# A reordered first phase in a retention, ELU and maxout chain on one core

## The chip, the core and the metric

The kernel runs on one core of a Trainium2 chip. TensorE (PE) multiplies matrices into PSUM, VectorE (DVE), ScalarE (ACT) and GpSimd (POOL) work element by element, SyncE (SP) issues most transfers from memory. Each engine takes its own instructions strictly in order; semaphores hold an instruction back until what it needs is there. The metric is the device time of the kernel in microseconds, as a median of runs. One more execution was profiled, and all rows come from that one.

## The reference, cut to what matters

```python
# 4 batches, 8 heads, 768 tokens, 64 wide; gamma and scale are constants
for t in range(S):                                   # retention
    state = gamma * state + outer(k[:, :, t], v[:, :, t])
    y[:, :, t] = scale * (q[:, :, t] @ state)
x = y as (3072 tokens, 512)
h = x @ w_in                                         # 512 -> 2048
g = where(h > 0, h, exp(min(h, 0)) - 1)              # ELU
x = g @ w_out                                        # 2048 -> 512
h = max(x @ w1, x @ w2, x @ w3)                      # 512 -> 768, maxout
out = h @ w_out2                                     # 768 -> 512
```

The weights are float64 in memory.

## The kernel before

**Retention by chunks.** A chunk is 128 tokens of one batch, all heads; there are 24. For a chunk TensorE makes scores (keys by queries), VectorE multiplies them with a decay mask (`a`), TensorE multiplies the masked scores with the values and adds what the state of earlier chunks gives (`past`). The outer products of decayed keys (`kd`) and values go into the next state (`update` on TensorE, `carry` on VectorE and GpSimd). GpSimd also scales queries (`queries_of`, `qd`) and keys (`keys_of`, `kd`). The result of four chunks is one block `x` of 512 tokens, held as a high part `xh` (rounded by ScalarE) and a low part `xl` (the rest, by VectorE). Chunks 0 to 3 go through the `wide_` functions (heads in one piece of 128), later ones through `open_chunk` (scores, update, mask), `values`, `finish` and `ready` (carry, `qd`, the next `kd`), in pieces of 64. In `values`, ScalarE writes a `guard` column that the second part of `past`, in `finish`, waits for.

**Weights.** A weight of the first layer, number f of 16, is 128 columns of `w_in` and 128 rows of `w_out`, and comes in two halves of 512 KB: half 2f for `w_in`, half 2f + 1 for `w_out`. Float64 is taken apart by hand: `cv_bits(n)` (ScalarE, L337), `cv_rest(n)` (VectorE, three operations, L344, L347 and L350), `cv_high(n)` (ScalarE, L361), `cv_low(n)` (VectorE, L366). A raw half lies in one of two buffers (`stage`), and `cv_rest(n)` issues the load of half n + 2.

**Steps.** `h1(b, f)` multiplies weight f with block b (12 matmuls of 512 columns into `hp`, L396); ScalarE and VectorE make ELU of it, `Exp`, `Relu`, `e` (L403, L404, L407), and split it into `gh` (ScalarE, L408) and `gl` (VectorE, L411). `o1(b, f)` multiplies these with the other half of the weight into four accumulators `acc` (12 matmuls, L430). A step is one `h1` and one `o1`; in the loop `h1` of the next step stands ahead of `o1`. Steps run in groups (b, from f, to f): a group accumulates, and at its end `x2_out` takes the accumulators away. Blocks 0 and 1 share the first 32 steps, so that a weight is used twice while the next ones are converted: before, in seven groups, with partial sums kept in a tile (`part`) and added to at the end of later groups. `third` puts chunks 8 to 11 between steps 14 and 31.

**What sets the order.** On TensorE, VectorE, ScalarE, GpSimd and SP the order of this phase is the order of the code, until the last block of the first layer; from there a scheduler decides. Loads go through one queue of SP, in order.

Of the kernel before, what the change touches and what calls it, by code (L numbers as in the profile page):

```python
# [34 lines left out]
def kernel(ctx: ExitStack, tc: tile.TileContext, qkv0, qkv, wa, wb, dmask, qdec, cols, out):  # L35
# [221 lines left out]
    def wide_scores(c):  # L257
        x = raw_t[c]
        sc = sc_t[c] = [ps_acc.tile([P, NPAIR, P], F32, tag="acc", name="sc") for _ in range(2)]
        for p in range(NPAIR):  # L260
            for r in range(2):
                nc.tensor.matmul(
                    sc[r][:, p, :], x[rows(r), p, 1, :], x[rows(r), p, 0, :], start=p == 0, stop=p == NPAIR - 1
                )

    def wide_mask(c):
# [3 lines left out]
        for r in range(2):  # L270
            nc.vector.tensor_tensor(
                out=a[:, r], in0=sc[r], in1=dmask_sb.rearrange("j (p r) i -> j r p i", r=2)[:, r], op=ALU.mult
            )
# [163 lines left out]
    def x2_out(b, f0, f1, keep):  # L437


        if b < 2:  # L440
            if b not in part_t:
                part_t[b] = ld.tile([P, KDM, BLK], F32, tag="r", name="part")
            o = part_t[b]
            o = o if isinstance(o, list) else [o[:, m] for m in range(KDM)]
            for m in range(KDM):
                if f0:
                    nc.vector.tensor_tensor(out=o[m], in0=acc_t[b][m], in1=o[m], op=ALU.add)
                elif m % 2 == 0:
                    nc.scalar.copy(o[m], acc_t[b][m])
                else:  # L450
                    nc.vector.tensor_copy(o[m], acc_t[b][m])
                if not keep:
                    nc.sync.dma_start(out=x2d[m, :, b * BLK:(b + 1) * BLK], in_=o[m])
            if not keep:
                del part_t[b]
# [289 lines left out]
    for c in range(CB):  # L745
        wide_scores(c)
        wide_mask(c)
        if c == 0:
            junk(8)
        if c == 2:  # L750
            cv_bits(0)
            cv_rest(0)
            load(5)
        if c == 3:
            cv_high(0)
            wide_rest(2)
            cv_low(0)
        if c:
            queries_of(c)
# [233 lines left out]
```

## Time and profile before

| | us |
|---|---|
| median of 3 runs | 1018.33 (1015.37 to 1021.66) |
| the profiled execution | 1016.3 |
| its span | 1014.5 |
| TensorE busy | 985.0 (97%) |
| VectorE busy | 606.2 (60%) |
| ScalarE busy | 348.9 (34%) |
| GpSimd busy | 67.1 (7%) |

The span is the time from the first to the last instruction that the profile shows. Matmuls are pipelined and overlap, so a busy TensorE is not yet one at its peak; idle time of an engine is what no instruction covers, and the profile says what ended it. The granted clock is the share of its full 2.4 GHz that TensorE had.

### The profile page before, as it was taken

The numbers are of one execution on the slowest core, as the hardware profiler recorded it, in microseconds if no ns is written. First come the engines' busy times: TensorE is split into PE (matmuls) and PEld (weight loads), VectorE is DVE, ScalarE is ACT, GpSimd is POOL, SyncE is SP. The second block draws the span as 40 slices with busy tenths as digits, with TensorE's granted clock in tenths as the row PEclk, the third lists the DMA queues.
The fourth block names the chain that finished last, engine by engine and source line by source line (L and its number), as shares of the span: only waits on it lengthen the run. The fifth ranks groups of instructions, "written<-read, shape, count | busy, mean of one in ns | idle before, by whom it ended". The sixth has DMA issues, their size and how long they took to land.

```text
span 1014.5 us, 18210 instructions
## 1 busy us (share of the span) xinstructions
PE 985.0 (97%) x7616; PEld 841.5 (83%) x7616; DVE 606.2 (60%) x1187; ACT 348.9 (34%) x669; POOL 67.1 (7%) x68
## 2 busy tenths in 40 slices
PE   7889999999999999999999999999999999999997
PEld 4667887777888888888888887888999999899996
DVE  2867888744333323333335887997875676757764
ACT  1445555533333333333334665432221121211211
POOL 2410001021111110111100000000000000000000
PEclk9999999999999999999999999999999999999999
DMA  9913364454211211121102444302001020110101
GB/s 236 237 59 103 104 188 161 136 182 127 88 43 43 84 43 42 43 84 43 43 1 87 143 145 146 105 1 83 2 26 58 2 78 6 42 43 1 43 1 42
DMA packets 59010, 79.70 MB, mean 79 GB/s; under 512 B 5168, under 2 KB 40240, under 8 KB 58928
## 3 DMA queue, kind: packets, MB, share of 16 engines
q1 hardware_dynamic: 53168, 68.05, 22.7%
q10 hardware_dynamic: 5760, 10.49, 2.8%
q8 instruction: 60, 0.98, 0.4%
q14 instruction: 22, 0.18, 0.1%
HBM read 63.84 MB, written 14.68 MB: 77 GB/s over the span
## 4 chain that ended last, share of the span: by engine, by line
PE 74%; DVE 13%; DMA 5%; ACT 4%; issue 2%; SPq 1%; POOL 1%; ACTq 0%; DVEq 0%; POOLq 0%
PE hp L612 19%; PE hp L396 19%; PE acc L430 19%; PE acc L661 8%; PE hp L501 5%; DMA raw<-in_wb 3%; DVE t L347 2%; DVE xl L586 1%; ACT gh L408 1%; DVE t L350 1%; DVE e L407 1%; DVE t L619 1%; PE xs L217 1%; PE xs L160 1%; DVE gl L411 1%
## 5 line engine op out<-in xcount | busy, mean ns | idle before, releaser
L396 PE MATMUL hp<-xh,w 128*128 128x512 f32 x768 | 243.7, 390 | 3.8 <-ACT w L361 2.9
L612 PE MATMUL hp<-xh,w 128*128 128x256 f32 x1260 | 232.5, 283 | 2.0 <-DVE e L619 1.6
L430 PE MATMUL acc<-gh,w 128*128 128x512 f32 x768 | 206.4, 397 | 5.6 <-ACT gh L408 3.1
L612 PEld LDWEIGHTS hp<-xh,w 128*128 128x128 f32 x1260 | 198.1, 191 | 4.0 <-issue 1.4
L612 PE MATMUL hp<-xl,w 128*128 128x256 f32 x630 | 178.9, 284 | 1.4 <-DVE xl L586 1.4
L430 PEld LDWEIGHTS acc<-gh,w 128*128 128x128 f32 x768 | 142.7, 189 | 39.8 <-ACT gh L408 4.6
L396 PEld LDWEIGHTS hp<-xh,w 128*128 128x128 f32 x768 | 143.7, 188 | 35.3 <-ACT w L361 4.3
L407 DVE SCALAR_TENSOR_TENSOR e<-e,hp 128x512 f32<-128x512 f32 x96 | 65.8, 685 | 175.9 <-ACT e L404 175.2
L396 PE MATMUL hp<-xl,w 128*128 128x512 f32 x384 | 141.9, 390 | 0.7 <-DVE xl L252 0.7
L612 PEld LDWEIGHTS hp<-xl,w 128*128 128x128 f32 x630 | 120.0, 191 | 4.2 <-DVE xl L586 2.9
L403 ACT ACTIVATE e<-hp 128x512 f32<-128x512 f32 x96 | 57.2, 596 | 171.7 <-PE hp L396 169.2
L430 PE MATMUL acc<-gl,w 128*128 128x512 f32 x384 | 110.9, 390 | 0.3 <-DVE gl L411 0.3
L411 DVE TENSOR_TENSOR gl<-e,gh 128x512 fp32r<-128x512 f32 x96 | 67.3, 701 | 55.9 <-ACT gh L408 54.9
L661 PE MATMUL acc<-w,gh 128*128 128x512 f32 x288 | 90.6, 391 | 0.0
L408 ACT CAST gh<-e 128x512 fp32r<-128x512 f32 x96 | 59.5, 619 | 81.0 <-DVE e L407 79.3
L619 DVE TENSOR_TENSOR t<-hp,m 128x256 f32<-128x256 f32 (+1 forms) x90 | 45.9, 510 | 68.7 <-PE hp L612 68.1
L396 PEld LDWEIGHTS hp<-xl,w 128*128 128x128 f32 x384 | 72.0, 188 | 16.3 <-DVE xl L252 1.0
L430 PEld LDWEIGHTS acc<-gl,w 128*128 128x128 f32 x384 | 72.2, 188 | 16.0 <-DVE gl L411 0.8
L631 ACT COPY m<-hp 128x256 f32<-128x256 f32 x45 | 16.8, 373 | 189.0 <-PE hp L612 115.0
L661 PEld LDWEIGHTS acc<-w,gh 128*128 128x128 f32 x288 | 53.9, 188 | 10.0
L404 ACT ACTIVATE e<-e 128x512 f32<-128x512 f32 x96 | 60.7, 632 | 2.8
L661 PE MATMUL acc<-w,gl 128*128 128x512 f32 x144 | 56.5, 392 | 1.0 <-DVE gl L651 1.0
(100 smaller groups left out, 1048.3 us busy)
## 6 DMA issues: line engine op xcount, KB each, us to landing
...
```

The costliest lines, as they stand in the source:

```text
L347: nc.vector.scalar_tensor_tensor(out=t, in0=hi, scalar=-0x80000000, in1=t, op0=ALU.bitwise_and, op1=ALU.bitwise_or)
L396: nc.tensor.matmul(hp, w[:, pw, kk * P:(kk + 1) * P], x[px][:, kk, :], start=k == 0, stop=k == len(order) - 1,)
L403: nc.scalar.activation(e, hp, ACTF.Exp)
L404: nc.scalar.activation(e, e, ACTF.Relu, scale=-1.0, bias=1.0)
L407: nc.vector.scalar_tensor_tensor(out=e, in0=e, scalar=-1.0, in1=hp, op0=ALU.mult, op1=ALU.max)
L408: nc.scalar.copy(gh, e)
L411: nc.vector.tensor_tensor(out=gl, in0=e, in1=f32(gh), op=ALU.subtract)
L430: nc.tensor.matmul(acc_t[b][m], w[:, p[0], 512 + m * P:512 + (m + 1) * P], g[p[1]], start=f == f0 and p == first, stop=f == f1 - 1 and p = ...
L501: nc.tensor.matmul(hp, w[:, pw, c0:c0 + P], x[px][:, kk, :], start=k == 0, stop=k == 3 * KDM - 1)
L612: nc.tensor.matmul(o, ws[i][:, pw, kk * P:(kk + 1) * P], xs[i][px][:, kk, :], start=first and k == 0, stop=last and k == 5,)
L619: nc.vector.tensor_tensor(out=out, in0=a, in1=c, op=ALU.add)
L661: nc.tensor.matmul(acc_t[NB + b][m], g[px][:, m * P:(m + 1) * P], w[:, pw, 512:1024], start=f == 0 and i == 0, stop=f == KF2 - 1 and i == 2,)
```

## The change

It rewrites the first phase, up to step 31.

- The wide chunks: scores go into four accumulators and are masked in four pieces; `update` stands ahead of the mask, and the state is made apart (`wide_state`).
- Chunks 4 to 7 go one at a time between `h1(0, k)` and `o1(0, k)`, for k of 2 to 5 (a "cycle" below); before, several of them stood between the first two steps.
- Two halves are converted in each of these cycles, so that a new weight is ready for each step of block 0.
- Blocks 0 and 1 take turns in four groups: 7, 9, 9 and 7 steps. The sums of the first two groups go to memory and come back by `renew`.
- Halves of weights whose f is no multiple of 3 (below 12) are loaded into the pool `ld` in pairs; so up to six halves are on their way. `dmask` is loaded ahead of the second part of chunk 0, the halves 0, 2, 1, 3 behind chunk 3.

```diff
     def wide_scores(c):
-        sc = sc_t[c] = [ps_acc.tile([P, NPAIR, P], F32, tag="acc", name="sc") for _ in range(2)]
+        sc = sc_t[c] = [[ps_acc.tile([P, 2, P], F32, tag="acc", name="sc") for _ in range(2)] for _ in range(2)]
...
     def load_half(n):
+        f, cc = n // 2, slice(n % 2 * 512, (n % 2 + 1) * 512)
+        if f % 3 and f < 12:
+            if f not in pairs_of:
+                pairs_of[f] = ld.tile([P, 2, 512, 2], I32, tag="r", name="raw")
+            r = pairs_of[f][:, n % 2]
+        else:
             r = stage.tile([P, 512, 2], I32, tag="raw", name="raw")
...
+    def load_next(n):
+        f = n // 2
+        if f % 3 and f < 12:
+            if n % 2 and f + 3 < 12:
+                load_half(n + 5)
+                load_half(n + 6)
+        elif f < 12:
+            load_half(n + 6)
+        else:
+            load_half(n + 2)
...
-    groups = [(0, 0, 2), (1, 0, 4), (0, 2, 6), (1, 4, 8), (0, 6, 11), (1, 8, KFF), (0, 11, KFF)]
+    groups = [(0, 0, 7), (1, 0, 9), (0, 7, KFF), (1, 9, KFF)]
...
+    nc.sync.dma_start(out=dmask_sb, in_=dmask)
     load(0, 1)
-    nc.sync.dma_start(out=dmask_sb, in_=dmask)
     load(1)
     nc.sync.dma_start(out=qdec_sb, in_=qdec)
     load(2)
-    load_half(0)
     load(3)
-    load_half(1)
+    for h in (0, 2, 1, 3):
+        load_half(h)
     load(4)
+    load_half(4)
+    load_half(5)
+    load(5)
...
     for c in range(CB):
         wide_scores(c)
+        wide_update(c)
+        if c == 0:
+            junk(7)
         wide_mask(c)
-        if c == 0:
-            junk(8)
...
-    h1(0, 0, [(ready, 4), (cv_bits, 2)], [(cv_low, 1)], [(open_chunk, 4), (cv_high, 1)])
-    values(4)
-    cv_rest(2)
-    o1(0, 0, 0, 2)
-    open_chunk(5)
-    finish(4)
-    ready(5)
...
+    h1(0, 0, [(cv_low, 1)], [], [(cv_high, 1)])
+    cv_bits(3)
+    later(False)
+    nc.scalar.copy(dmask_sb[rows(1), :, 0:HC], dmask_sb[rows(1), :, HC:P])
+    cv_rest(3)
+    load(7)
+    h1(0, 1, [(cv_low, 3)], [], [(cv_high, 3)])
+    o1(0, 0, 0, 7)
+    open_chunk(4)
+    o1(0, 1, 0, 7)
+    cv_bits(4)
+    cv_rest(4)
+    cv_high(4)
+    ready(4)
+    cv_bits(5)
+    cv_low(4)
+    cv_rest(5)
+    for k in range(2, 6):
+        h1(0, k, [(cv_low, 2 * k + 1)], [], [(cv_high, 2 * k + 1)])
+        c = k + 2
+        values(c)
+        if c + 1 < EARLY:
+            open_chunk(c + 1)
+        finish(c)
+        if c + 1 < EARLY:
+            ready(c + 1)
+        o1(0, k, 0, 7)
+        cv_bits(2 * k + 2)
+        cv_rest(2 * k + 2)
+        cv_high(2 * k + 2)
+        cv_bits(2 * k + 3)
+        cv_low(2 * k + 2)
+        cv_rest(2 * k + 3)
+    h1(0, 6, [(cv_low, 13)], [], [(cv_high, 13)])
...
+        if i == split - 11:
+            renew(0)
```

VectorE before, around chunks 5 and 6 and the step (0, 1): `e` and `gl` are ELU of that step, `w<-t,w` is `cv_low`, `a` the mask of a chunk, `xl` its low part, `dmask_sb` and `state` its carry, `t` the pieces of `cv_rest`.

```order
L407 SCALAR_TENSOR_TENSOR e<-e,hp 128x512 [waits Activation_49]
L411 TENSOR_TENSOR gl<-e,gh 128x512 [waits Activation_49]
L366 TENSOR_TENSOR w<-t,w 128x512
L172 TENSOR_TENSOR a<-xs,dmask_sb 128x256 [waits PE_49] x2
L252 TENSOR_TENSOR xl<-xs,xh 128x4x64 [waits Activation_49] x2
L200 COPY dmask_sb<-xs 128x4x64
L207 TENSOR_TENSOR state_90<-xs,dmask_sb 128x256 [waits DVE_49]
L172 TENSOR_TENSOR a<-xs,dmask_sb 128x256 [waits PE_49] x2
L252 TENSOR_TENSOR xl<-xs,xh 128x4x64 [waits Activation_49] x2
L205 TENSOR_TENSOR dmask_sb<-xs,dmask_sb 128x4x64 [waits Pool_49]
L207 TENSOR_TENSOR state_91<-xs,dmask_sb 128x256 [waits DVE_49]
```

VectorE now, from `e` of the step (0, 3), in the cycle k = 3; the names are the same.

```order
L427 SCALAR_TENSOR_TENSOR e<-e,hp 128x512 [waits Activation_49]
L386 TENSOR_TENSOR w<-t,w 128x512 [waits Activation_49]
L431 TENSOR_TENSOR gl<-e,gh 128x512 [waits Activation_49]
L172 TENSOR_TENSOR a<-xs,dmask_sb 128x256 [waits PE_49] x2
L252 TENSOR_TENSOR xl<-xs,xh 128x4x64 [waits Activation_49] x2
L200 COPY dmask_sb<-xs 128x4x64
L207 TENSOR_TENSOR state_90<-xs,dmask_sb 128x256 [waits DVE_49]
L364 TENSOR_SCALAR t<-t 128x512 [waits Activation_49]
L367 SCALAR_TENSOR_TENSOR t<-raw,t 128x512 [waits DMAHW7_49,DVE_49]
L370 SCALAR_TENSOR_TENSOR t<-raw,t 128x512 [waits DVE_49]
L386 TENSOR_TENSOR w<-t,w 128x512 [waits Activation_49]
```

One chunk stands behind a step, where two stood, and the conversion of the next weight stands behind that chunk, in the same cycle.

TensorE now, from the end of `o1(0, 1)` into the cycle k = 2: `acc` is `o1`, `hp` is `h1`, `xs<-a,x` the values of chunk 4.

```order
L450 MATMUL acc<-gh,w 128x512 x4
L416 MATMUL hp<-xh,w 128x512 [waits Activation_49]
L416 MATMUL hp<-xh,w 128x512 x3
L416 MATMUL hp<-xl,w 128x512 x4
L416 MATMUL hp<-xh,w 128x512 [waits DVE_49]
L416 MATMUL hp<-xh,w 128x512 x3
L230 MATMUL xs<-a,x 64x64
```

TensorE before, from the end of `finish(4)` into `h1(0, 1)` and the values of chunk 5:

```order
L396 MATMUL hp<-xh,w 128x512 [waits DVE_49,Activation_49]
L396 MATMUL hp<-xh,w 128x512 x3
L396 MATMUL hp<-xl,w 128x512 x4
L396 MATMUL hp<-xh,w 128x512 [waits DVE_49]
L396 MATMUL hp<-xh,w 128x512 x3
L230 MATMUL xs<-a,x 64x64 [waits PE_49]
```

In both, `h1` begins behind a wait for ScalarE (`cv_high`). Now this comes once in each cycle, directly behind `o1` of the cycle before.

SP before, from the last part of chunk 2 on (`x` is a chunk, `raw` a half of a weight):

```order
L102 DMA x<-in_qkv 128x4x256
L324 DMA raw<-in_wa 128x1024
L86 DMA x<-in_qkv 64x4x128 x2
L86 DMA x<-in_qkv 64x4x256
L102 DMA x<-in_qkv 128x4x256
L324 DMA raw<-in_wa 128x1024
```

SP now, from the same place:

```order
L102 DMA x<-in_qkv 128x4x256
L86 DMA x<-in_qkv 64x4x128 x2
L86 DMA x<-in_qkv 64x4x256
L102 DMA x<-in_qkv 128x4x256
L335 DMA raw<-in_wa 128x1024 x4
```

Half 0 moved from ahead of chunk 3 to behind it, and three more halves follow it.

## Rows read from the trace of the kernel before

**Rows 1.** Three stretches: length, busy time of each engine, granted clock, DMA.

```profile
0.00:86.30 86.30, 71.83 (x902) 53.89 (x903) 52.18 (x94) 29.07 (x58) 20.63 (x22) 0.98 0.66 169
86.30:218.50 132.20, 129.03 (x733) 103.77 (x732) 101.27 (x167) 69.57 (x122) 7.84 (x7) 1.00 0.47 150
218.50:1014.50 796.00, 784.12 (x5983) 683.86 (x5982) 452.79 (x927) 250.21 (x490) 38.66 (x39) 1.00 0.18 57
```

**Rows 2.** Waits of TensorE up to 230 us: total, times, longest.

```profile
PE xo L282 <- DVE a L271: 5.7, 8, 2.7
PE hp L396 <- ACT w L361: 2.9, 4, 1.3
```

**Rows 3.** Timeline of TensorE: start, duration, operation, [idle before, releaser].

```profile
32.35 1.19 PE L396 MATMUL hp<-xh,w 128*128 128x512 f32 x4
...
45.08 1.21 PE L396 MATMUL hp<-xh,w 128*128 128x512 f32 x4 [1.28 <-ACT w L361]
...
48.07 0.69 PE L230 MATMUL xs<-a,x 64*64 64x64 f32 x32
...
50.21 0.63 PE L160 MATMUL xs<-x 64*64 64x64 f32 x27 [0.88 <-DVE e L407]
...
51.76 0.74 PE L430 MATMUL acc<-gh,w 128*128 128x512 f32 x2
...
83.62 0.39 PE L396 MATMUL hp<-xh,w 128*128 128x512 f32 x1
...
86.34 1.07 PE L430 MATMUL acc<-gh,w 128*128 128x512 f32 x4
```

**Rows 4.** Timelines of ScalarE (half 0) and GpSimd (keys of chunk 3).

```profile
23.80 0.69 ACT L337 ACTIVATE t<-raw 128x512 f32<-128x512 f32 x1 [2.53 <-DMA raw<-in_wa]
...
28.25 1.04 POOL L138 TENSOR_TENSOR kd<-x,cols_sb 128x512 f32<-128x512 f32 x1 [4.24 <-DMA x<-in_qkv]
```

**Rows 5.** Timeline of VectorE: first and last piece of one `cv_rest`.

```profile
59.44 0.43 DVE L344 TENSOR_SCALAR t<-t 128x512 int32<-128x512 int32 x1 [1.65 <-ACT t L337]
...
60.62 0.69 DVE L350 SCALAR_TENSOR_TENSOR t<-raw,t 128x512 uint32<-128x512 uint32 x1
```

**Rows 6.** Timeline of ScalarE behind `h1` at 45.08: `Exp` and a `cv_high`.

```profile
48.17 0.60 ACT L403 ACTIVATE e<-hp 128x512 f32<-128x512 f32 x1 [2.57 <-PE hp L396]
...
49.43 0.63 ACT L361 CAST w<-t 128x512 fp32r<-128x512 f32 x1
```

**Rows 7.** Timeline of VectorE behind the same `h1`.

```profile
49.47 0.69 DVE L407 SCALAR_TENSOR_TENSOR e<-e,hp 128x512 f32<-128x512 f32 x1 [0.56 <-ACT dmask_sb L240]
50.84 0.69 DVE L411 TENSOR_TENSOR gl<-e,gh 128x512 fp32r<-128x512 f32 x1 [0.69 <-ACT gh L408]
51.45 0.68 DVE L366 TENSOR_TENSOR w<-t,w 128x512 fp32r<-128x512 f32 x1
52.05 0.75 DVE L172 TENSOR_TENSOR a<-xs,dmask_sb 128x256 f32<-128x256 f32 x2
...
53.83 0.42 DVE L207 TENSOR_TENSOR state<-xs,dmask_sb 128x256 f32<-128x256 f32 x1
```

**Rows 8.** Timelines of GpSimd and VectorE where keys and `cv_rest` meet.

```profile
45.68 1.49 POOL L138 TENSOR_TENSOR kd<-x,cols_sb 128x512 f32<-128x512 f32 x1
...
46.19 1.26 DVE L344 TENSOR_SCALAR t<-t 128x512 int32<-128x512 int32 x1
```

**Rows 9.** Stretches as in rows 1; the granted clock is third from the end.

```profile
12.90:16.30 3.40, 3.31 (x34) 3.19 (x36) 0.49 (x3) 0.59 (x1) 0.46 (x1) 0.50 1.14 247
40.00:60.00 20.00, 17.68 (x418) 14.01 (x416) 14.73 (x30) 6.49 (x18) 7.83 (x8) 1.00 0.61 153
623.80:627.30 3.50, 3.50 (x9) 2.72 (x10) 3.42 (x7) 2.57 (x5) 0.00 (x0) 0.51 0.55 156
```

**Rows 10.** Timeline of TensorE at two long waits.

```profile
12.39 0.43 PE L282 MATMUL xo<-a,x 128*64 128x128 f32 x2 [2.70 <-DVE a L271]
...
623.73 3.68 PE L430 MATMUL acc<-gh,w 128*128 128x512 f32 x8 [2.10 <-ACT gh L408]
```

More of the change, by code (lines that the diff above doesn't have):

```diff
@@ L262, in wide_scores @@
                 nc.tensor.matmul(
[L263 removed]
+                    sc[p // 2][r][:, p % 2, :], x[rows(r), p, 1, :], x[rows(r), p, 0, :],
+                    start=p % 2 == 0, stop=p % 2 == 1,
                 )
@@ L269, in wide_mask @@
         sc, a = sc_t.pop(c), wide[0][:, c % 2]
[L270 to L273, printed above, removed]
+        d = dmask_sb.rearrange("j (p r) i -> j r p i", r=2)
+        for k in range(2):
+            pp = slice(2 * k, 2 * k + 2)
+            for r in range(2):
+                nc.vector.tensor_tensor(out=a[:, r, pp], in0=sc[k][r], in1=d[:, r, pp], op=ALU.mult)
         a_t[c] = a
@@ L435, with x2_out @@
     part_t = {}
[L437 to L455, printed above, removed]
+    def x2_out(b, f0):
+        if b < 2 and f0:
+            for m, o in enumerate(part_t.pop(b)):
+                nc.vector.tensor_tensor(out=o, in0=acc_t[b][m], in1=o, op=ALU.add)
+                nc.sync.dma_start(out=x2d[m, :, b * BLK:(b + 1) * BLK], in_=o)
             del acc_t[b]
@@ L746 @@
         wide_scores(c)
+        wide_update(c)
+        if c == 0:
+            junk(7)
         wide_mask(c)
-        if c == 0:
-            junk(8)
-        if c == 2:
+        if c:
+            queries_of(c)
+        keys_of(c + 1)
+        wide_state(c)
+        if c:
+            wide_rest(c - 1)
+        if c == 3:
             cv_bits(0)
             cv_rest(0)
[L753 to L759, printed above, removed]
@@ L760 @@
-        if c + 1 < CB:
-            keys_of(c + 1)
-        wide_mix(c)
-        wide_update(c)
-        if c != 2:
-            wide_rest(c)
-    keys_of(4)
+        wide_mix(c)
+    cv_high(0)
+    wide_rest(3)
+    cv_low(0)
+    cv_bits(2)
+    cv_rest(2)
+    load(6)
+    cv_bits(1)
+    cv_high(2)
+    cv_rest(1)
+    cv_low(2)
+    h1(0, 0, [(cv_low, 1)], [], [(cv_high, 1)])
+    cv_bits(3)
+    later(False)
     nc.scalar.copy(dmask_sb[rows(1), :, 0:HC], dmask_sb[rows(1), :, HC:P])
-    cv_bits(1)
@@ L769 @@
-    later(False)
-    cv_rest(1)
-    load(6)
+    cv_rest(3)
     load(7)
-    h1(0, 0, [(ready, 4), (cv_bits, 2)], [(cv_low, 1)], [(open_chunk, 4), (cv_high, 1)])
-    values(4)
-    cv_rest(2)
-    o1(0, 0, 0, 2)
-    open_chunk(5)
-    finish(4)
-    ready(5)
-    cv_high(2)
-    cv_low(2)
-    cv_bits(3)
-    cv_rest(3)
-    h1(0, 1, [], [(cv_low, 3), (open_chunk, 6), (finish, 5), (ready, 6)], [(values, 5), (cv_high, 3)])
-    o1(0, 1, 0, 2, (0, 1))
-    values(6)
-    open_chunk(7)
-    finish(6)
@@ L789 @@
-    ready(7)
-    o1(0, 1, 0, 2, (2,))
-    values(7)
+    h1(0, 1, [(cv_low, 3)], [], [(cv_high, 3)])
+    o1(0, 0, 0, 7)
+    open_chunk(4)
+    o1(0, 1, 0, 7)
     cv_bits(4)
     cv_rest(4)
-    o1(0, 1, 0, 2, (3,))
-    finish(7)
-    h1(1, 0, [(cv_high, 4)], [(cv_bits, 5)])
-    x2_out(0, 0, 2, True)
+    cv_high(4)
+    ready(4)
+    cv_bits(5)
     cv_low(4)
     cv_rest(5)
-    n = 5
+    for k in range(2, 6):
[14 more added lines that the diff above has]
+        cv_rest(2 * k + 3)
@@ L802, in renew @@
+    h1(0, 6, [(cv_low, 13)], [], [(cv_high, 13)])
+    cv_bits(14)
+    cv_rest(14)
+    n = 14
     def renew(b):
@@ L824, in third @@
             swap()
-            renew(0)
         if i == split - 2:
@@ L876 @@
             if f == f1 - 1:
-                x2_out(b, f0, f1, f1 < KFF and (b, f0) not in parked)
+                x2_out(b, f0)
         if converting:
```

31 lines of the change are left out of this document (16 added, 15 removed).

## The prediction

> **What bounds the kernel now.** First I cut the span into stretches [rows 1]. In the first 86.30 us TensorE is busy for 71.83, so it idles 14.5 us; from there to 218.5 it idles 3.2 (132.20 - 129.03); in the last 796 us it idles 12. TensorE is the bound nearly everywhere, and only its idle time can be won. From 218.5 on, the order of TensorE and VectorE is the same row for row in both kernels, so the change can move the time in the first two stretches alone, and I leave the third as it is.
>
> Then the waits of TensorE [rows 2] say on what it idles there: `w` of ScalarE (`cv_high`) and the masked scores of VectorE. So the first phase is a chain through VectorE, with TensorE behind it.
>
> As a milestone I take 86.34 us [rows 3]. There chunks 0 to 7 are done, and so are seven `h1` and five `o1`: twelve blocks of 12 matmuls. Without a wait a block takes 2.72 us (83.62 to 86.34). In the changed order the same work (chunks 0 to 7, twelve blocks) is done when `h1(0,6)` begins. So the question is when that is, against 86.34, and what is won back behind it.
>
> **The start.** SP issues 1 MiB for a chunk and 0.5 MiB for a half of a weight. Before, half 0 ends at 4.25 MiB of the list and is first used at 23.80, chunk 3 ends at 5.25 and its keys start at 28.25 [rows 4]: 4.45 us per MiB. The new list has chunk 3 at 4.75 (so 26.0 us), half 0 at 5.25 (28.25), half 2 at 30.5, half 1 at 32.7. Before, `h1(0,0)` came 4.1 us behind the keys of chunk 3 (28.25 to 32.35) [rows 3, 4]; that would give 30.1 now, but half 0 lands later than before: 28.25, +0.69 for `cv_bits` [rows 4], +1.87 for `cv_rest` (59.44 to 60.62 + 0.69) [rows 5], +0.63 for `cv_high` [rows 6] = 31.45. So `h1(0,0)` starts at 31.5, 0.85 us earlier than 32.35. Two edits I cost at nothing here. The masks in four pieces instead of two, with `up` ahead of them, shorten a chunk's chain, but the landings set the pace. The products of chunk 0 wait for `dmask`, now 0.5 MiB ahead of its keys (2.2 us later); the later landings cover that. Without the cover it is up to 2 us late.
>
> **From there VectorE is full.** In the new order stand, between 31.45 and the end of `cv_rest(4)`, eight passes over 512 columns (four `cv_low`, two `e`, two `gl`) at 0.60 (51.45 to 52.05 [rows 7]), four `cv_rest` at 1.80 from start to start, `later` at 0.65 (estimated as one such pass), a mask pair at 0.67: 4.8 + 7.2 + 0.65 + 0.67 = 13.3, and some 0.35 of waiting for ScalarE. With the end of `cv_rest` (0.08) and `cv_high(4)` (0.65) this makes 45.85 for the start of `h1(0,2)`.
>
> **The cycles.** Now the term on which all rests. In cycle k (2 to 5) VectorE works through `e`, `cv_low(2k+1)`, `gl`, mask, `xl`, carry, `cv_rest(2k+2)` in this order; then ScalarE's `cv_high(2k+2)` releases `h1(0,k+1)`. Before, nearly the same row of work stands at 45.08 to 54.25: from the start of `h1` [rows 3] through `Exp` at 48.17 and `Relu` behind it [rows 6], `e` at 49.47, `gl`, `cv_low`, mask to the end of the carry at 53.83 + 0.42 [rows 7], 9.17 us. Now `cv_low` lies in the wait between `e` and `gl`, which takes off 0.60. `cv_rest` (1.87), `cv_high` (0.66 with its start) and 0.05 to TensorE come on top: 11.15 us. Cycle 5 has no mask and no carry and waits for `xh` instead: about 10.3.
>
> TensorE needs less in a cycle: two blocks, 5.44, and `values`, `open_chunk`, `finish`, 2.81 (48.07 to 51.76 less a wait of 0.88 [rows 3]), 8.25 together. It idles near 3 us in each cycle, in two pieces: some 1.4 ahead of `finish` (whose `guard` copies stand behind `gh` on ScalarE) and about 2 ahead of the next `h1`. Loads don't set the pace: 2 MiB in a cycle are 8.9 us.
>
> **GpSimd.** In cycles 2 and 3 the keys of the next chunk start on GpSimd when `cv_rest` starts on VectorE. The one place before where they met: keys at 45.68 took 1.49 against 1.04 at 28.25, and the `cv_rest` piece at 46.19 took 1.26 against 0.43 [rows 4, 5, 8]. I add 1.0 us in these two cycles; nothing and 1.0 in all four are the bounds. The Trainium skill's page "SBUF — State Buffer", section "Who interferes with whom", says that an instruction of VectorE with two inputs in SBUF, or in a two-port mode, and one of GpSimd that reads SBUF lock each other out for a whole instruction. By that rule each of the four cycles could lose a pass of GpSimd, and the sum would be 2 us above mine; the row at 46.19 agrees, for one meeting.
>
> So `h1(0,6)` begins at 45.85 + 12.15 + 12.15 + 11.15 + 10.3 = 91.6, which is 5.3 us behind 86.34.
>
> **Won back behind it.** From here the seven `h1` of block 1 need no conversion, and conversions end five steps earlier (step 20 against 25). VectorE loses 12 of 28 passes over accumulators (0.6 each, 7 us), since there are four groups of steps and not seven. Of the 3.2 us of idle between 86.3 and 218.5 I take back all but 0.75, as one change of group still stands near the end: -2.45; the bounds are 0 and -3.2. The eight copies and stores at the first two ends of groups are hidden by the `h1` block of 2.72 us that stands ahead of the next `o1`; uncovered they are two copies, 1.3 us, each. `renew` of block 0 comes eight steps earlier than before: three steps, 16 us, ahead of its use, against landings of a few us.
>
> **The clock.** After a wait of 2.10 us at 623.73 the granted clock was 0.51 for the next 3.5 us, after one of 2.70 at 12.39 it was 0.50, the lower level of 1.2 GHz [rows 9, 10]; the wait of 1.28 at 45.08 left it at 1.00, the level of 2.4 GHz [rows 3, 9]. The waits ahead of `h1(0,3)` and `h1(0,4)` come to some 2.8 us with GpSimd's share. I count one fall: eight matmuls at about 0.43 instead of 0.23, 1.6 us on the chain. Bounds: none, and four, 6.4.
>
> **The sum.** 5.3 - 2.45 + 1.6 = +4.4 us against the profiled execution's 1016.3 (1014.5 of span and 1.8 around it), 1020.7. The median of the runs shown, 1018.33, is 2.0 above the profiled one, so 1022.7; I say 1022.5.
>
> **Rivals.**
> (a) Clearly slower: every cycle's `h1` starts at the low clock and GpSimd holds up every `cv_rest`. That is 3 x 1.6 + 2 x 1.0 = 6.8 above my sum: 1029.5. For it: the waits come back each cycle, at the same place. Against: only two are over 2.1 us. It decides when a cycle takes 13.3 us or more on average. 0.13.
> (b) Faster: VectorE's conversions run ahead, and the cycles go at TensorE's 8.25. Then `h1(0,6)` begins at 45.85 + 4 x 8.25 = 78.9, 7.5 ahead of before, and with 3.2 won back the time is 1018.3 - 10.7 = 1007.6. For it: VectorE is busy for only about 8.1 of 11 us (two `cv_rest` 3.6, four passes 2.4, mask, `xl` and carry 2.1). Against: its order is written out, and `cv_rest(2k+2)` stands behind `e` of the same cycle, which needs `h1(0,k)`. 0.05.
> (c) The chain as I see it, but won back in full: the start 2 us earlier, no fall of the clock, no meeting with GpSimd, 3.2 us regained. 89.6 - 2.0 - 86.34 - 3.2 is -1.9: 1016.4, within 1%. 0.2.
> (d) The change only reorders and the sum is as above: my forecast. 0.62, own range 1018 to 1027.
>
> About 1% (10 us) is what a measurement of this kernel can tell from no change. Faster by more (1008 or less) is (b): 0.05. Slower by more (1028.5 or above) is (a) and a little of (d): 0.15. Within: 0.8. The range from (c) less 3 to (a) plus 2, 1013 to 1032, leaves out (b) and the ends of (a).
>
> **What would show it.** In the profile after: `h1(0,0)` near 31.5; the starts of `h1(0,2)` to `h1(0,6)` 10 to 12 us apart, each released by ScalarE's cast into `w`; `h1(0,6)` near 91.6; TensorE idle about 3 us in each cycle, and nearly none from there to 218. A granted clock under 1.00 between 40 and 92 us is the term of the clock. I am wrong if the starts of `h1` lie 8 to 9 us apart (then (b)), if they are released by loads, or if the idle time behind 92 us stays.

## The result and the profile after

| | before | after |
|---|---|---|
| median of 20 runs each, us | 1016.70 (1012.09 to 1021.66) | 1021.92 (1017.84 to 1025.23) |
| ratio | | 1.0051, 95% interval 1.0035 to 1.0067 |
| the profiled execution, us | 1016.3 | 1022.84 |
| its span, us | 1014.5 | 1021.1 |

The changed kernel is 5.2 us longer. The interval leaves out 1, so the difference is real, but it is within the 1% that the prediction calls no change. Its median is 0.6 from the 1022.5 that was predicted. That is closer than the working deserves: the median of three runs from which it started, 1018.33, lies 1.6 above the one of twenty, one term was wrong by 2.7 us, and 2.2 us came back in a stretch that the prediction left as it is. The traces show where.

First the stretches, as in [rows 1], with the same columns (length; busy time of PE, PEld, DVE, ACT, POOL; granted clock; DMA). I cut at the milestone (86.34 before; now the start of `h1(0,6)`, 97.30) and at the first matmul of `values(9)`, the first place where the order is the same in both kernels (218.60 before, 227.37 now).

Stretches of after:

```profile
0.00:97.30 97.30, 74.25 (x901) 55.16 (x902) 62.00 (x117) 33.58 (x66) 20.22 (x22) 0.91 0.75 193
97.30:227.37 130.07, 127.94 (x732) 104.28 (x732) 84.49 (x140) 65.81 (x115) 7.74 (x7) 1.00 0.42 130
227.37:1021.10 793.73, 782.27 (x5983) 682.87 (x5982) 452.22 (x927) 249.74 (x490) 38.55 (x39) 1.00 0.18 55
```

The second and the third of before, cut at the same places:

```profile
86.34:218.60 132.26, 129.09 (x733) 103.77 (x731) 101.23 (x167) 69.65 (x122) 7.84 (x7) 1.00 0.48 150
218.60:1014.50 795.90, 784.01 (x5983) 683.86 (x5982) 452.79 (x927) 250.13 (x489) 38.66 (x39) 1.00 0.18 57
```

The same work on TensorE (901 matmul records, 902 in [rows 1]) ends 10.96 us later at the milestone; 2.19 come back up to `values(9)` (132.26 - 130.07), which leaves 8.77; 2.17 more come back in the last stretch (795.90 - 793.73), where the two orders are the same. The sum is the 6.6 us between the spans. The granted clock of the first stretch is 0.91, where [rows 1] have 0.98.

The waits of TensorE in after, up to 230 us (total, times, longest), against [rows 2]:

```profile
PE hp L416 <- ACT w L381: 8.2, 6, 2.1
PE up L310 <- POOL kd L138: 6.8, 2, 5.7
PE acc L450 <- ACT gh L428: 4.2, 3, 2.2
PE xs L160 <- DVE e L427: 2.7, 3, 0.9
PE xs L217 <- ACT dmask_sb L240: 1.8, 1, 1.8
```

The masked scores are gone from the list. In their place stands a wait of 5.7 us for the keys of chunk 0, which ends at 12.75; `h1(0,0)`, which needs half 0, still comes at 32.38, before at 32.35. `hp <- w`, `h1` behind the cast `cv_high`, has grown from 2.9 to 8.2 us: the chain through VectorE and ScalarE. These rows of TensorE's timeline (start, duration, operation, [idle before, releaser]) are the first matmuls of `h1(0,0)`, `o1(0,1)`, `h1(0,2)` to `h1(0,6)` and, far behind, one `o1` at 121.03:

```profile
32.38 0.96 PE L416 MATMUL hp<-xh,w 128*128 128x512 f32 x3 [1.67 <-ACT w L381]
...
44.87 2.08 PE L450 MATMUL acc<-gh,w 128*128 128x512 f32 x4 [2.22 <-ACT gh L428]
...
49.47 1.20 PE L416 MATMUL hp<-xh,w 128*128 128x512 f32 x4
...
61.21 1.50 PE L416 MATMUL hp<-xh,w 128*128 128x512 f32 x4 [2.07 <-ACT w L381]
...
74.37 1.20 PE L416 MATMUL hp<-xh,w 128*128 128x512 f32 x4 [1.88 <-ACT w L381]
...
86.85 1.19 PE L416 MATMUL hp<-xh,w 128*128 128x512 f32 x4 [1.46 <-ACT w L381]
...
97.30 1.21 PE L416 MATMUL hp<-xh,w 128*128 128x512 f32 x4 [0.95 <-ACT w L381]
...
121.03 2.11 PE L450 MATMUL acc<-gh,w 128*128 128x512 f32 x8 [1.33 <-ACT gh L428]
```

The four cycles are 11.74, 13.16, 12.48 and 10.45 us, and the `h1` that ends each is released by the cast into `w`, as foreseen. But `h1(0,2)` came at 49.47 and not at 45.85. VectorE and GpSimd show why: the place is `ready(4)` and `cv_rest(3)`, `cv_rest(4)`, before the first cycle.

VectorE of after, 29 to 48 us:

```profile
29.20 0.68 DVE L302 TENSOR_TENSOR xl<-xo,xh 128x512 fp32r<-128x512 f32 x1
29.80 0.42 DVE L364 TENSOR_SCALAR t<-t 128x512 int32<-128x512 int32 x1
...
39.39 1.01 DVE L132 TENSOR_TENSOR qdec_sb<-qdec_sb,cols_sb 128x256 f32<-128x256 f32 x1
40.31 0.83 DVE L364 TENSOR_SCALAR t<-t 128x512 int32<-128x512 int32 x1
41.18 1.65 DVE L367 SCALAR_TENSOR_TENSOR t<-raw,t 128x512 int32<-128x512 int32 x1
42.87 0.69 DVE L370 SCALAR_TENSOR_TENSOR t<-raw,t 128x512 uint32<-128x512 uint32 x1
...
46.58 1.46 DVE L367 SCALAR_TENSOR_TENSOR t<-raw,t 128x512 int32<-128x512 int32 x1
```

GpSimd of after, the same time:

```profile
38.62 1.48 POOL L138 TENSOR_TENSOR kd<-x,cols_sb 128x512 f32<-128x512 f32 x1 [9.13 <-DMA x<-in_qkv]
40.07 0.79 POOL L202 TENSOR_TENSOR dmask_sb<-state,cols_sb 128x256 f32<-128x256 f32 x1
40.83 1.46 POOL L149 TENSOR_TENSOR qd<-x,qdec_sb 128x512 f32<-128x512 f32 x1
46.44 1.04 POOL L138 TENSOR_TENSOR kd<-x,cols_sb 128x512 f32<-128x512 f32 x1 [4.16 <-DMA x<-in_qkv]
```

Of what VectorE does while GpSimd runs `kd(4)`, the state, `qd` and `kd(5)`, four instructions are drawn out. From start to start, L132 takes 0.92 where it takes 0.34 with GpSimd idle (e3_gpsimd_idle, below), L364 0.87 for 0.46, and the two L367 1.69 and 1.49 for 0.73: 0.58 + 0.41 + 0.96 + 0.76 = 2.7 us.

The granted clock fell to 0.50 three times on the way (columns as above, the clock third from the end). Stretches of after:

```profile
44.90:48.30 3.40, 3.40 (x8) 2.73 (x9) 3.33 (x7) 0.49 (x1) 1.04 (x1) 0.50 1.09 254
61.90:65.30 3.40, 3.40 (x10) 2.63 (x9) 1.70 (x3) 0.00 (x0) 0.00 (x0) 0.50 0.57 194
75.60:79.00 3.40, 3.40 (x16) 2.19 (x18) 1.20 (x2) 0.11 (x1) 0.00 (x0) 0.50 0.27 77
```

Each fall stands behind one of the waits above: 2.22, 2.07 and 1.88 us. The first slowed `o1(0,1)`, which ended only just ahead of `h1(0,2)`; ScalarE's cast for that `h1` (48.79 to 49.41) was done no sooner, so this fall cost nothing here.

### The profile page after: what moved, and what is told of

It is laid out like the page before. It is cut to its first block, busy times and chain, and to the rows that moved or that the text cites. A ratio compares the mean times of both kernels' runs of the same rounds, so it can differ in the third digit from the quotient of the medians.

```text
span 1021.1 us, 18193 instructions
## 1 busy us (share of the span) xinstructions
PE 984.5 (96%) x7614; PEld 842.3 (82%) x7615; DVE 598.7 (59%) x1183; ACT 349.1 (34%) x669; POOL 66.5 (7%) x68
## 4 chain that ended last, share of the span: by engine, by line
PE 76%; DVE 11%; DMA 6%; ACT 4%; issue 2%; SPq 0%; POOL 0%; ACTq 0%; DVEq 0%; POOLq 0%
PE hp L416 21%; PE acc L450 20%; PE hp L620 19%; PE acc L669 8%; PE hp L509 5%; DMA raw<-in_wb 3%; DMA x<-in_qkv 2%; DVE t L367 2%; DVE xl L594 1%; DVE t L370 1%; DVE t L627 1%; PE xs L217 1%; PE xs L160 1%; ACT gh L428 1%; PE xs L230 1%
## 5 line engine op out<-in xcount | busy, mean ns | idle before, releaser
L450 PE MATMUL acc<-gh,w 128*128 128x512 f32 x768 | 203.4, 396 | 6.5 <-ACT gh L428 6.1
L627 DVE TENSOR_TENSOR t<-hp,m 128x256 f32<-128x256 f32 (+1 forms) x90 | 45.9, 510 | 69.2 <-PE hp L620 68.4
```

The lines of the kernel that those rows point to most:

```text
L450: nc.tensor.matmul(acc_t[b][m], w[:, p[0], 512 + m * P:512 + (m + 1) * P], g[p[1]], start=f == f0 and p == first, stop=f == f1 - 1 and p = ...
L627: nc.vector.tensor_tensor(out=out, in0=a, in1=c, op=ALU.add)
```

## Experiments

Theory: the order sets a cycle. `cv_rest(2k+2)` stands behind `e` of the same cycle, so each `h1` waits for a chain through VectorE, which GpSimd and the clock lengthen. The rival is amount: VectorE (or the loads) has too much to do in a cycle, whatever the order.

"h1(0,2) to h1(0,6)" is read from TensorE's timeline of each run. The first three rows have the same order up to 94 us; d2_pass_in_gap adds work that proved free, and e7_rest_first differs at the start. Falls outside 40 to 101 us are not in the last column: e3_gpsimd_idle and e1_again each have one near 31 us, in `h1(0,0)`.

| | h1(0,0) | h1(0,2) | four cycles | h1(0,6) | values(9) | span | clock falls, 40 to 101 |
|---|---|---|---|---|---|---|---|
| after | 32.38 | 49.47 | 11.74 13.16 12.48 10.45 | 97.30 | 227.37 | 1021.1 | 44.9, 61.9, 75.6 |
| after_again | 33.27 | 50.27 | 11.60 13.18 12.20 10.44 | 97.69 | 228.15 | 1021.8 | 45.9, 62.9, 76.6 |
| e5_sp_stores | 32.13 | 48.70 | 11.71 12.85 11.03 10.46 | 94.75 | 223.87 | 1017.6 | 61.9 |
| d2_pass_in_gap | 30.79 | 46.95 | 11.74 11.59 12.61 10.46 | 93.35 | 222.98 | 1016.6 | 70.8 |
| e7_rest_first | 30.19 | 47.56 | 11.72 11.58 12.61 10.44 | 93.91 | 223.54 | 1017.2 | 71.7 |
| d1_pass_on_chain | 33.11 | 48.95 | 12.04 12.21 13.51 12.84 | 99.55 | 231.29 | 1024.7 | 73.0, 86.6, 100.3 |
| e2_filled | 32.70 | 49.83 | 11.72 11.61 11.06 10.46 | 94.68 | 225.30 | 1021.5 | none |
| e2_filled_again | 31.58 | 48.90 | 11.72 11.58 11.04 10.46 | 93.70 | 226.28 | 1021.9 | none |
| e3_gpsimd_idle | 31.21 | 46.87 | 10.73 11.22 11.02 10.46 | 90.30 | 220.30 | 1014.8 | none |
| e1_rest_early | 31.33 | 48.23 | 9.53 9.40 9.25 9.19 | 85.60 | 214.32 | 1010.0 | none |
| e1_again | 31.75 | 49.23 | 9.50 9.38 9.25 9.19 | 86.55 | 215.36 | 1009.4 | none |
| e6_best | 32.62 | 49.19 | 9.50 9.37 9.25 9.19 | 86.50 | 215.48 | 1010.6 | none |
| e8_best_start | 30.74 | 47.89 | 9.53 9.38 9.24 9.20 | 85.24 | 214.23 | 1007.9 | none |

### The conversion one step earlier: e1_rest_early and e1_again

The one part undone on which the prediction rests: `cv_rest(2k+2)` stands ahead of `h1(0,k)` instead of behind `finish`.

```diff
     for k in range(2, 6):
+        cv_bits(2 * k + 2)
+        cv_rest(2 * k + 2)
         h1(0, k, [(cv_low, 2 * k + 1)], [], [(cv_high, 2 * k + 1)])
...
         finish(c)
+        cv_high(2 * k + 2)
+        cv_bits(2 * k + 3)
...
         o1(0, k, 0, 7)
-        cv_bits(2 * k + 2)
-        cv_rest(2 * k + 2)
-        cv_high(2 * k + 2)
-        cv_bits(2 * k + 3)
         cv_low(2 * k + 2)
         cv_rest(2 * k + 3)
-    h1(0, 6, [(cv_low, 13)], [], [(cv_high, 13)])
...
+    cv_bits(14)
     cv_rest(14)
+    h1(0, 6, [(cv_low, 13)], [], [(cv_high, 13)])
```

> The changed kernel with one thing moved: in each cycle k the conversion of the next half, cv_bits and cv_rest(2k+2), stands ahead of e of step (0,k) on VectorE, in the 2 us in which VectorE waits for h1, instead of behind the carry. Nothing is added or left out. Theory (the serial chain h1, e, gl, mask, xl, carry, cv_rest, cv_high sets the cycle, not the amount of work): the starts of h1(0,2) to h1(0,6) lie 9 to 9.5 us apart instead of 10.5 to 13.2, h1(0,6) begins near 87 instead of 97.3, and the time falls by 8 to 10 us from that of the changed kernel, to 1011 to 1014. Rival (the waits come from VectorE and GpSimd locking each other out and from the falls of the clock): neither is touched, the cycles stay at 11 to 13 us and the time within 2 us of 1021.9.

> e1_rest_early once more, as the partner of e6_best and e8_best_start on one chip. The same theory as before: cv_rest ahead of h1 takes the conversion out of the chain, so cycles of 9.2 to 9.6 us and h1(0,6) about 54.3 us behind h1(0,0); ratio 0.994 to 0.999.

Measured: 1012.61 us, ratio to before 0.9968 (0.9947 to 0.9990), and again 1012.78, 0.9968 (0.9949 to 0.9988): by the ratios some 8.4 us under after (1.0051 - 0.9968), and under before too. TensorE's timeline of e1_rest_early at `h1(0,2)` to `h1(0,6)`:

```profile
48.23 1.21 PE L416 MATMUL hp<-xh,w 128*128 128x512 f32 x4 [1.50 <-ACT w L381]
...
57.76 1.07 PE L416 MATMUL hp<-xh,w 128*128 128x512 f32 x4
...
67.16 1.07 PE L416 MATMUL hp<-xh,w 128*128 128x512 f32 x4
...
76.41 1.07 PE L416 MATMUL hp<-xh,w 128*128 128x512 f32 x4
...
85.60 1.07 PE L416 MATMUL hp<-xh,w 128*128 128x512 f32 x4
```

From `h1(0,3)` on there is no wait ahead of `h1`, with the same instructions on every engine and the same loads. The order set the cycle. Most of what a cycle still has over the 8.25 of TensorE's own work that the prediction summed is one wait of 0.9 to 1.0 for `e` (2.8 us in three), ahead of the scores of the next chunk, and in cycle 5 the 1.8 for the `guard`.

### The same work in two places: d1_pass_on_chain and d2_pass_in_gap

After, with two passes of VectorE over a scratch tile in each cycle: once ahead of `cv_bits(2k+2)`, on the chain (d1), once behind `cv_rest(2k+3)`, where VectorE waits for the next `h1` (d2).

```diff
         o1(0, k, 0, 7)
+        for _ in range(2):                    # d1
+            nc.vector.memset(dpool.tile([P, 512], F32, tag="m", name="m"), 0.0)
         cv_bits(2 * k + 2)
         cv_rest(2 * k + 2)
         cv_high(2 * k + 2)
         cv_bits(2 * k + 3)
         cv_low(2 * k + 2)
         cv_rest(2 * k + 3)
+        for _ in range(2):                    # d2
+            nc.vector.memset(dpool.tile([P, 512], F32, tag="m", name="m"), 0.0)
```

> The changed kernel with two passes of VectorE (memset of 512 columns, about 0.55 us each) added in each of the four cycles, between the carry and cv_rest(2k+2). If the chain sets the cycle: h1(0,6) begins 4 to 4.5 us later than 97.3. If VectorE has room (it is busy for 8 of 12 us): nothing.

> After, with two extra passes of VectorE over 512 columns (memsets of a scratch tile) in each cycle k = 2 to 5, put behind cv_rest(2k+3), where VectorE has nothing to do until the next h1 is there. In d1_pass_on_chain the same two passes stood ahead of cv_bits(2k+2), on the chain. My theory: the order is what sets a cycle, so passes in the gap are free: h1(0,6) within 1 us of after's 97.3. Rival: VectorE's amount of work sets the cycle; then each cycle is longer by about the two passes (0.5 to 0.6 each by d1's difference), and h1(0,6) is 2 to 4.5 us later.

VectorE of d1, behind the carry of cycle 2 and again in cycle 3:

```profile
57.28 1.02 DVE L809 MEMSET m<- 128x512 f32 x2
58.22 0.61 DVE L364 TENSOR_SCALAR t<-t 128x512 int32<-128x512 int32 x1
58.87 0.69 DVE L367 SCALAR_TENSOR_TENSOR t<-raw,t 128x512 int32<-128x512 int32 x1
```

VectorE of d2, ahead of `e` of cycle 3:

```profile
61.20 1.03 DVE L815 MEMSET m<- 128x512 f32 x2
63.04 0.69 DVE L427 SCALAR_TENSOR_TENSOR e<-e,hp 128x512 f32<-128x512 f32 x1 [0.81 <-ACT e L424]
```

Two passes are 0.94 us from start to start. In the gap they cost nothing: the cycles of d2 without a clock fall (11.74, 11.59 and 10.46) are those of the other runs to 0.02 us, since VectorE still waits 0.81 for ScalarE behind them. On the chain they cost all of it where nothing else changed: cycle 5 of d1 is 12.84, less some 1.4 for a clock fall (1.2 to 1.6, below) 11.4, against 10.46. In cycles 2 and 3 they cost 0.3 and 0.6, because L367 there now starts when GpSimd is done (0.69, where after has 1.41 at 58.37): the delay took the place of the meeting. So `h1(0,6)` of d1 came at 99.55, 2.3 us behind after and not the 4 to 4.5 expected: a miss. That of d2 came at 93.35, 4 us ahead of after and so outside what was expected too, since its `h1(0,2)` came 2.5 us sooner and one fall of the clock less stood in its cycles. Time was 1026.43 us for d1 and 1018.41 for d2, one execution each. An amount of VectorE's work that costs nothing in the gap does not set the cycle, and e1_rest_early has the same loads in the same order: the rival falls.

### GpSimd out of the way: e3_gpsimd_idle

After, with the scaling of keys and queries of chunks 4 to 7 by GpSimd left out.

```diff
     def keys_of(c):
+        if CB <= c < EARLY:
+            st_t.setdefault(c, [None, None])[1] = raw_t[c][:, :, 2, :].rearrange("t p (r d) -> t p r d", r=2)
+            return
...
     def queries_of(c):
+        if CB <= c < EARLY:
+            st_t.setdefault(c, [None, None])[0] = raw_t[c][:, :, 0, :]
```

> The changed kernel with the scaling of keys and queries of chunks 4 to 7 left out (raw keys and queries go into the products), so that GpSimd only has the small carry product there; VectorE's own work is the same. Theory (VectorE's stretched pieces at 39.4 to 43, 46.6 and 57.6 to 59.8, in sum 4.1 us over their usual length, are meetings with GpSimd): all pieces of cv_rest have their usual length, h1(0,2) begins 2.7 us earlier (46.8), h1(0,6) about 4 us earlier (93.3, less or more by a fall of the clock), time near 1018. Rival (they are stretched by something else, as the loads): they stay, and the time stays.

Measured: 1019.48 us, ratio 1.0029 (1.0007 to 1.0052), beside a median of before of 1015.19 on the same chip. From `h1(0,2)` to `h1(0,6)` it is 43.43 us against the 44.85 and 44.78 of the two runs that have GpSimd but no clock fall either (e2_filled, below): meetings are worth 1.4 us in the cycles. From `h1(0,0)` to `h1(0,2)` it is 15.66 against 17.09 in after. That is less than the 2.7 us of drawn-out instructions, for two reasons: one L367 is still drawn out a little beside the carry's product (1.01 from start to start for 0.73), and `e` of step (0, 0) waits 0.92 us for ScalarE, which in after it did not, as `h1(0,0)` ran at the lower clock here (2.07 for its first four matmuls, 1.20 in after).

TensorE of e3_gpsimd_idle at `h1(0,0)`, then VectorE at L132 (L370 here is L364 of after):

```profile
31.21 2.07 PE L422 MATMUL hp<-xh,w 128*128 128x512 f32 x4 [2.22 <-ACT w L387]
```

```profile
39.23 0.43 DVE L132 TENSOR_TENSOR qdec_sb<-qdec_sb,cols_sb 128x256 f32<-128x256 f32 x1
39.57 0.42 DVE L370 TENSOR_SCALAR t<-t 128x512 int32<-128x512 int32 x1
```

`h1(0,2)` came at 46.87, the 46.8 expected, but partly because `h1(0,0)` was 1.2 us earlier. GpSimd is a cause, and not the main one: without it each cycle is still a chain of 10.5 to 11.2 us.

### The clock: e2_filled, after_again, e2_filled_again

Filling matmuls into `hp` stand ahead of `h1(0,3)` to `h1(0,6)` (9, 9, 6 and 4 of them), so that TensorE works through the wait.

```diff
+        for i in range(fill):
+            nc.tensor.matmul(hp, w_t["a", f - 1][:, 0, 0:P], x[0][:, 0, :], start=i == 0, stop=i == fill - 1)
```

> The changed kernel with matmuls of no use ahead of h1(0,3) to h1(0,6) (9, 9, 6 and 4 of 512 columns, into the accumulator that h1 then starts anew), to keep TensorE at work in the wait for cv_high. Theory of the clock (two falls, at 61.9 and 75.6, cost 1.4 to 1.7 us each on the chain): no fall from 58 to 92 us, h1(0,6) about 3 us earlier (94), time near 1019. Rival (the falls lie where TensorE waits anyway): h1(0,6) stays at 97, time 1021 to 1022.5.

> The changed kernel once more, beside e2_filled_again and e5_sp_stores on the same chip. By my theory the cycles' clock falls are a habit of this order and not of one execution: the profile shows again two or three falls of the granted clock to 0.50 between 40 and 80 us, each behind a wait of about 1.9 to 2.2 us, and h1(0,6) within 0.7 us of 97.3. Rival: which waits are followed by a fall is chance; then h1(0,6) comes anywhere from 94.5 to 97.5. Time 1.003 to 1.007 of the kernel before by both.

> After, with filling matmuls ahead of h1(0,3) to h1(0,6), as in e2_filled, now beside after on the same chip. If the clock falls on the chain cost what the profile says (97.30 - 94.68 = 2.6 us at h1(0,6)) and nothing gives it back, the time is 2 to 3 us below that of after_again, a ratio of about 1.003 against 1.005 or 1.006. Rival: the saved time is lost later (a fall at a later wait, or TensorE waiting for what its extra matmuls delayed); then the two times agree within 1 us or e2 is longer, as the 1023.81 of the first run has it.

Measured: e2_filled 1023.81 us, ratio 1.0081 (1.0052 to 1.0110); later after_again 1021.48, 1.0046 (1.0028 to 1.0064), and beside it e2_filled_again 1024.36, 1.0065 (1.0041 to 1.0088). The falls in the cycles are gone and `h1(0,6)` comes 2.6 and 4.0 us sooner than in after and after_again (1.4 of the 4.0 stand already at `h1(0,2)`), but the time doesn't fall. In the profiled executions the gain is given back later, as the rival had it. e2_filled_again loses 2.1 us of it between `h1(0,6)` and `values(9)` (132.58 us, 130.46 in after_again), where one `o1` fell to the lower clock (0.50 to 0.51 from 119.5 on) behind a wait of 1.84 us; in after the wait there was 1.33. And both runs of e2 have a fall of the clock near 631.5 and a last stretch of 796.2 and 795.6 us, where after, after_again, e5 and d2 have 793.6 to 793.7.

TensorE of e2_filled_again at both places, then of after at the second, one `o1` behind nearly the same wait:

```profile
118.57 3.04 PE L452 MATMUL acc<-gh,w 128*128 128x512 f32 x8 [1.84 <-ACT gh L430]
...
631.37 3.68 PE L452 MATMUL acc<-gh,w 128*128 128x512 f32 x8 [1.94 <-ACT gh L430]
```

```profile
632.13 2.14 PE L450 MATMUL acc<-gh,w 128*128 128x512 f32 x8 [1.86 <-ACT gh L428]
```

The same eight matmuls take 3.68 or 2.14 us. The medians of e2 are 2 to 3 us above those of after, though on the same chip the intervals overlap; the profiles, whose spans are within 0.8 us of after's, don't explain that, and it stays open.

after_again was twice right by its theory (three falls, 97.69), but the other runs with this order side with its rival: e5_sp_stores, the same program up to 94 us, waited 1.88 us ahead of `h1(0,4)` as after did, and the clock did not fall:

```profile
73.26 1.20 PE L416 MATMUL hp<-xh,w 128*128 128x512 f32 x4 [1.88 <-ACT w L381]
```

Over the first five rows of the table the falls between 40 and 80 us are 3, 3, 1, 1 and 1. A fall in a cycle costs 1.2 to 1.6 us (13.16 and 12.85 against 11.59; 12.48, 12.20 and 12.61 against 11.03).

### The stores: e5_sp_stores

```diff
-            nc.scalar.dma_start(out=to, in_=o)
+            (nc.sync if b < 2 else nc.scalar).dma_start(out=to, in_=o)
```

> After, with the stores of the first two ends of groups issued by SP and not by ScalarE. My theory: the wait of 1.33 us that TensorE has at 121.03 for ScalarE's gh is left from the two stretches of 0.83 us that ScalarE spends issuing these stores (108.39 and 109.87), so Exp(1,1) starts about 0.9 us earlier and the wait falls to 0.5 us or less; idle time between h1(0,6) and 222 falls from 2.1 to about 1.3; time about 1 us under after. Rival: the double conversion at step 7 causes the wait; then it stays at 1.0 us or more.

ScalarE of after, where the first group ends (ACTq is ScalarE's queue issuing a transfer):

```profile
108.39 0.83 ACTq L476 DMA_DIRECT2D x2d<-o  x2
109.26 0.59 ACT L473 COPY o<-acc 128x512 f32<-128x512 f32 x1 [0.90 <-PE hp L416]
109.87 0.83 ACTq L476 DMA_DIRECT2D x2d<-o  x2
110.75 0.60 ACT L423 ACTIVATE e<-hp 128x512 f32<-128x512 f32 x1 [0.91 <-DVE t L367]
```

ScalarE of e5 at the same place:

```profile
105.23 1.05 ACT L473 COPY o<-acc 128x512 f32<-128x512 f32 x2
106.31 0.60 ACT L423 ACTIVATE e<-hp 128x512 f32<-128x512 f32 x1
```

Without the 1.7 us of issuing, the next `Exp` follows the copies at once. The wait of 1.33 us at 121.03 becomes

```profile
117.45 2.12 PE L450 MATMUL acc<-gh,w 128*128 128x512 f32 x8 [0.30 <-ACT gh L428]
```

Counted from the start of `h1(0,6)`, `values(9)` comes after 129.12 us and not 130.07. So in this order 1.0 of the 1.33 was the stores. The stores alone don't make the wait: e1_again leaves them on ScalarE and waits 0.25 there. The 0.30 that is left is put down to the double conversion of step 7; e6_best, which moves it (below), has no such wait there. Measured 1020.68 us, ratio 1.0032 (1.0013 to 1.0051), against 1.0046 for after_again on the same chip: of the expected size, but the intervals overlap.

### The start: e7_rest_first

`cv_bits(0)` and `cv_rest(0)` ahead of `wide_state(3)` and `wide_rest(2)`.

```diff
+        if c == 3:
+            cv_bits(0)
+            cv_rest(0)
         wide_state(c)
         if c:
             wide_rest(c - 1)
-        if c == 3:
-            cv_bits(0)
-            cv_rest(0)
```

> After, with cv_rest(0) ahead of the state of chunk 3 and the low part of chunk 2 on VectorE. My theory: the start of h1(0,0) was late because cv_rest(0) stands behind these two and not because half 0 landed late; so from cv_bits(0) to h1(0,0) it is 3.2 to 3.4 us in place of 4.1 (28.27 to 32.38), as my prediction worked it out. But VectorE has the same work up to h1(0,2), so from cv_bits(0) to h1(0,2) it is at most 0.5 us less than the 21.2 of after. Rival: the start matters further on, and h1(0,2) too comes 0.8 us earlier or more, measured from cv_bits(0).

Measured (one execution, 1018.94 us): `cv_bits(0)` at 25.70, `cv_rest(0)` at 27.18, `h1(0,0)` at 30.19. That is 4.49 us from `cv_bits(0)`, where I expected 3.2 to 3.4: a miss. In this execution the half had landed early, and VectorE still had the masks of chunk 3 to do; then ScalarE's cast of `xh` (29.04) stood ahead of `cv_high` (29.52). Second part: from `cv_bits(0)` to `h1(0,2)` it is 21.86 us, no less than the 21.2 of after. The bound that I gave for it holds, but since the first step was no earlier by this count, whether one would be passed on was not tested. The reason I gave for its lateness was only one of three that lie close together.

### The best version: e6_best and e8_best_start

e6_best is e1_rest_early with the stores of e5_sp_stores and the double conversions at steps 9, 11 and 13 (`if i in (9, 11, 13)` for `(7, 11, 15)`); e8_best_start adds the edit of e7_rest_first.

> e1_rest_early plus two more edits: the first two ends of groups are stored by SP, and the steps that convert two halves at once are 9, 11 and 13 and not 7, 11 and 15. My theory: e1's cycles of 9.2 to 9.5 us stay, TensorE's waits for gh between h1(0,6) and 222 (1.0 us in e1) fall to 0.3 or less, span within 1 us of 1009.3, time 0.5 to 1 us under e1_again. Rival: other waits for w come in where the double conversions now stand (0.5 us or more), and the time is e1's.

> e6_best plus the edit of e7_rest_first. By my theory the start gains nothing that reaches h1(0,2), and the time is that of e6_best within 0.5 us; by the rival it is 0.8 us less.

Measured: e6_best 1011.36 us, ratio to before 0.9958 (0.9937 to 0.9978); e8_best_start 1012.21, 0.9963 (0.9942 to 0.9984); e1_again, beside them, 0.9968. The waits for `gh` between `h1(0,6)` and 222 did not fall: 1.2 us in e6 against 0.9 in e1_again, now behind the double conversions of steps 9 and 11 (0.46 at 130.95 and 0.78 at 142.90). They moved with the conversions. All three are faster than before by 0.3 to 0.4%; which of them is best, and so whether the edit of the start is worth anything, can't be told from these runs.

## Why the prediction came out as it did

**Chain and cycles: right.** The term on which all rested holds. Where no fall of the clock came, the cycles are 11.7, 11.6, 11.03 and 10.45 us; predicted were 12.15, 12.15, 11.15 and 10.3. TensorE idles 2.4 to 3.0 us in a cycle of after, near the 3 foreseen; but the first piece, 0.9, stands ahead of the next chunk's scores and waits for `e`, not for the `guard` (this only in cycle 5, 1.75). e1_rest_early shows that the cause is the order, and d2 that VectorE's load is not. That the four cycles together came within 0.5 us (47.83 for 47.35 with the one fall) is in part luck: two falls cost 3.0 for 1.6, meetings 1.4 for 2.0, and the chain without either is 43.43 (e3_gpsimd_idle) for 43.75. Rival (b), conversions that run ahead, failed for the reason given against it, and e1_rest_early is what that rival would have needed.

**From `h1(0,0)` to `h1(0,2)`: mis-sized.** This is the step that failed: 14.35 us were summed, 17.09 measured in after. I had priced meetings with GpSimd "in cycles 2 and 3" alone, and every instruction of this earlier stretch at its undisturbed duration. But the same `keys_of` and `queries_of`, with the carry's state, stand there for chunks 4 and 5, beside `cv_rest(3)` and `cv_rest(4)`: 2.7 us. Other executions of this order show the same with other sizes, as chunks 4 and 5 land at other times: the drawn-out instructions, counted as above, add up to 1.65 us in d1, 1.83 in d2, 2.40 in e5, 2.79 and 2.97 in the two e2, for stretches of 15.84, 16.16, 16.57, 17.13 and 17.32. Without them all six, after too, come to 14.2 to 14.4. So the sum was right but for this term. In after_again (17.00) they are 2.0, and 0.6 more is the clock: the `o1(0,1)` that fell at 45.9 held up `h1(0,2)` there.

VectorE and GpSimd of d1, where the second L367 was over before `kd(5)` began:

```profile
46.83 0.69 DVE L367 SCALAR_TENSOR_TENSOR t<-raw,t 128x512 int32<-128x512 int32 x1
```

```profile
47.68 1.47 POOL L138 TENSOR_TENSOR kd<-x,cols_sb 128x512 f32<-128x512 f32 x1 [5.14 <-DMA x<-in_qkv]
```

**GpSimd in the cycles: a little high.** 2.0 us were summed for cycles 2 and 3, 1.4 measured; cycle 2 has its 1.0 as priced (the pair L364 and L367 at 57.64 takes 0.73 + 1.45 for 0.46 + 0.73). With the stretch before it is 4.1 us in all. The Trainium skill's page "SBUF — State Buffer", section "Who interferes with whom", says that an instruction of VectorE with two inputs in SBUF and one of GpSimd that reads SBUF lock each other out. The trace agrees as far as both are drawn out where they meet (L367 1.65 for 0.69, `kd` 1.48 for 1.04). The estimate that I drew from that rule, a pass lost in each of the four cycles and a sum 2 us above mine, does not come out: cycles 4 and 5 lost nothing (11.02 and 10.46 with GpSimd idle, 11.06 and 10.46 without a fall otherwise). That 4.1 is near its 4.0 is chance, as 2.7 of it lie ahead of the cycles.

**The clock: one fall counted, three in this execution.** The two of them in the cycles cost 1.6 and 1.45 us; the first, at 44.9, cost nothing. Those two came behind waits of 2.07 and 1.88 us, shorter than the 2.10 of [rows 10] by which I had weighed them and than the 2.8 that I had summed. In three of the five executions of nearly this order one fall came, as counted. The bounds (none to four) held.

**The start: close.** `h1(0,0)` was to come at 31.5. It came between 30.19 and 33.27 in the runs of the table, where `cv_bits(0)`, which needs half 0, began anywhere from 25.7 to 29.2. In after half 0 came at 28.27, as worked out (28.25), but `cv_rest(0)` began 0.83 us behind the end of `cv_bits(0)`, since on VectorE the state of chunk 3 and `xl` stand ahead of it; I had looked only at what the half itself must pass.

**Won back: right in sum, by luck in its parts.** 2.45 were predicted, 2.19 measured. The idle time left behind the milestone is 2.1 us, though, not 0.75, so that only 1.04 of 3.17 was won (the prediction named idle time that stays as a sign against it). That the eight copies and stores are hidden was wrong by 1.0 us (e5_sp_stores). The other 1.15 us is TensorE's busy time (129.09 to 127.94), of which the prediction says nothing; why it fell, no run shows.

**The rest of the program: assumed unchanged.** The order is, and the time was 2.17 us less. Most of this is the fall of the clock behind 623.73 [rows 9, 10], 1.5 us over the eight matmuls, which a like wait (1.86 for 2.10) did not bring about in after. It is this that hides most of the missing 2.7 us in the total, and it is luck: e2_filled and e2_filled_again, with the same order there, have the fall.

So the sum of the profiled execution, 1020.7, was 2.1 too low against 1022.84: 0.9 at the start, 2.7 behind it, 0.5 in the cycles and 0.3 in what is won back, less the 2.2 of the last stretch. Of rival (a), the falls of the clock came in part and the meetings where it did not look; its condition, 13.3 us a cycle on average, was not met (47.83 / 4 = 11.96).
